# Moving pieces of a weight load and the bias loads to other places in the DMA queues of a fused attention and MLP kernel

## The chip, the cores and the metric

The kernel runs on one core of a Trainium2 chip. The metric is the device time of one execution in microseconds (us); the time of a kernel is the median of its runs. The core has five engines with queues of their own: TensorE (PE, with its weight loads shown as PEld), VectorE (DVE), ScalarE (ACT), GpSimd (POOL) and SyncE (SP). In this kernel SP issues nearly all DMAs; ScalarE issues a few.

## The reference

The kernel computes a gated mix of two branches over one sequence of S = 2048 rows with D = 512 columns, all in bfloat16. The first branch is linear attention with 32 heads of 16 columns; the second mixes tokens with a two-layer MLP of F = 1792 hidden units along the sequence.

```python
def _A_ref(x, wqkv, wo):                    # x [1, 2048, 512]
    q, k, v = ...                           # x @ wqkv, split in 32 heads of 16
    phi = lambda t: jnp.where(t > 0, t + 1, jnp.exp(t)) + 1e-6
    pq, pk = phi(q), phi(k)
    kv = jnp.einsum("bhsd,bhse->bhde", pk, v)
    z = jnp.einsum("bhsd->bhd", pk)
    num = jnp.einsum("bhqd,bhde->bhqe", pq, kv)
    den = jnp.einsum("bhqd,bhd->bhq", pq, z)[..., None] + 1e-6
    return merge_heads(num / den) @ wo

def _B_ref(x, w1, b1, w2, b2):              # w1 [2048, 1792], w2 [1792, 2048]
    h = _layernorm(x, axis=-1)
    u = _gelu(jnp.einsum("bsd,sf->bdf", h, w1) + b1)
    y = jnp.einsum("bdf,fs->bds", u, w2) + b2
    return y.transpose(0, 2, 1)

g = _sigmoid((x * gate_w).sum(-1, keepdims=True))
out = g * a + (1 - g) * b                   # a = _A_ref(A_x, ...), b = _B_ref(A_x, ...)
```

The input B_x is not used: both branches read A_x.

## The kernel before, in words

The sequence is cut into NT = 16 tiles of 128 rows, D into ND = 4 blocks of 128, and F into NF = 14 blocks of 128. All is kept in SBUF and nearly every instruction is put in program order by hand (`pin`), so the order in the source is the order in each engine's queue. The helper `load` (L122) issues every DMA, by default on SP's queue, so in the profile all DMA issues stand at line L123; all matmuls go through `mm` and stand at L74.

The stages follow one another on TensorE.

1. **Start.** VectorE fills `eps_t` (L113) and GpSimd fills `b_rows` (L114), a tile of 32 rows that will take the biases b1 (14 rows of 128) and b2 (16 rows). ScalarE's queue issues the load of the first 128 columns of w1's first tile, and then a dummy Sqrt (L134) that brings in its table. SP issues x tile by tile, alternating with the tiles of `w1A`, the first 8 blocks of w1's columns; the two bias loads come after w1's tile 4. TensorE runs 18 warm-up matmuls on constants.
2. **Layer norm and the first 8 blocks of the MLP.** For each x tile, VectorE takes the statistics, ScalarE the square root (`sd`), VectorE the reciprocal and the normalised tile `xh`. TensorE accumulates 8 PSUM banks `accA` over the 16 tiles, 8 matmuls for each tile and w1 tile. After tile 8, VectorE turns `b_rows` into columns and casts them into `b1_sb` and `b2_sb`.
3. **phi(k) and G = x^T phi(k)**, 16 tiles, with the sums z of phi(k).
4. **The other 6 blocks of the MLP** (`mlp1_block`, reading `w1B`) between the 16 tiles of q (`q_tile`), whose phi goes to `pq`. At its start SP issues the first half of w2 into the buffer of w1A. The gelu of each block gives `uT`.
5. **normalise(t)**: four VectorE instructions for each tile of phi(q), 12 of them in a row and the last four later; it divides by the denominator, weights with the gate's odds, and ends with a store of the tile to DRAM (`q_dram`). **turn(c)** loads four tiles (a group) back transposed, in four transposing DMAs, into `pqT`. Both issue on SP. The second half of w2, `load_w2(1, ...)`, goes into the buffer of w1B, so it can't start before TensorE has finished stage 4's last block. It is issued in four pieces right after the store of tile 0.
6. **Output**: for each tile t, 14 matmuls of `uT` with w2 (`y_mm`, tiles 0 to 7 from w2's first half, 8 to 15 from the second) and 4 matmuls of `pqT` with the folded output weights (`a_mm`) accumulate in one PSUM bank `yps`. The order on TensorE is y_mm of tiles 0 to 7, a_mm of 0 to 7; then y_mm and a_mm of 8 to 11; then of 12 to 14; and tile 15 last, in two parts. `finish` scales on ScalarE (tile 15 on VectorE) and stores.

The buffers tie the stages together: `w1A` and w2's first half share one tag, `w1B` and w2's second half the other. PSUM has 8 banks under one tag, `ot` (the output tile) has 6 buffers.

Of the kernel before, what the change touches and what calls it, by code (L numbers as in the profile page):

```python
# [15 lines left out]
def kernel(  # L16
# [13 lines left out]
    nc = tc.nc  # L30
# [10 lines left out]
    NT = S // P  # L41
    ND = D // P
    NF = F // P
# [12 lines left out]
    b1_view = B_b1.rearrange("(f p) -> f p", p=P)  # L56
    b2_view = B_b2.rearrange("(t p) -> t p", p=P)
# [8 lines left out]
    def ptile(shape, dt, name):  # L66
        return persist.tile(shape, dt, name=name, tag=name)
# [27 lines left out]
    b_rows = ptile([32, P], BF16, "b_rows")  # L95
# [14 lines left out]
    z_cols = ptile([P, ND], FP32, "z_cols")  # L110
    eps_t = ptile([P, 1], FP32, "eps_t")

    nc.vector.memset(eps_t[:], EPS)  # L113
    nc.gpsimd.memset(b_rows[:], 0.0)  # L114


    w1A = wpool.tile([P, NT, FA], BF16, name="w1A", tag="w1st")
# [4 lines left out]
    def load(o, i, eng=None, **kw):  # L122
        pin((eng or nc.sync).dma_start(out=o, in_=i, **kw))  # L123

    def load_x(t0, t1):
        load(xr[:, t0:t1, :], x_view[:, t0:t1, :])

    def load_w1a(t):
        load(w1A[:, t, :], w1_view[:, t, 0:FA])


    tbl = work.tile([P, 1], FP32, name="tbl", tag="tbl", bufs=2)
    load(w1A[:, 0, 0:P], w1_view[:, 0, 0:P], nc.scalar)
    pin(nc.scalar.activation(out=tbl[:], in_=eps_t[:], func=ACT.Sqrt))  # L134

    load_x(0, 1)
# [2 lines left out]
    for t in range(1, NT):  # L139
        if t + 1 < NT:  # L140
            load_x(t + 1, t + 2)
        load_w1a(t)
        if t == 4:
            load(b_rows[0:NF, :], b1_view)
            load(b_rows[NF : NF + NT, :], b2_view)
    load(gw_b[:], gw_row_view.to_broadcast([P, D]))
    load(wk_sb[:], wqkv_view[:, :, D : 2 * D])
    for c in range(NSC):
# [240 lines left out]
    def normalise(t):  # L389
        heads = by_head(pq[:, t, :])  # L390
        pin(
            nc.vector.tensor_tensor(  # L392
                out=prod[:, :, 0:HEAD], in0=heads, in1=by_head(zb[:]), op=ALU.mult,
            )
        )
        den = work.tile([P, NH], FP32, name="den", tag="den", bufs=2)
        pin(nc.vector.tensor_reduce(out=den[:], in_=prod[:], op=ALU.add, axis=AX.X))  # L397
        rd = work.tile([P, NH], FP32, name="rd", tag="rd", bufs=2)
        pin(nc.vector.reciprocal(out=rd[:], in_=den[:]))  # L399
        pin(  # L400
            nc.vector.scalar_tensor_tensor(  # L401
                out=heads, in0=heads, scalar=odds[:, t : t + 1],
                in1=rd[:].unsqueeze(2).to_broadcast([P, NH, HEAD]),
                op0=ALU.mult, op1=ALU.mult,
            )
        )
        load(q_dram[t * P : (t + 1) * P, :], pq[:, t, :])

    def turn(c):
        for j in range(ND):  # L410
            load(
                pqT[:, j, c * SC : (c + 1) * SC],
                q_dram[c * SC : (c + 1) * SC, j * P : (j + 1) * P],
                transpose=True,
            )
# [33 lines left out]
    def load_w2(h, f0, n=7):  # L449
        if f0 == 0:  # L450
            w2s.append(wpool.tile([P, NF, S // 2], BF16, name="w2h", tag=("w1st", "w2nd")[h]))
        load(
            w2s[h][:, f0 : f0 + n, :],
            w2_view[:, f0 : f0 + n, h * (S // 2) : (h + 1) * (S // 2)],
        )
# [41 lines left out]
    pin(nc.vector.tensor_tensor(out=c2[:], in0=c1[:], in1=b2_sb[:], op=ALU.mult))  # L497


    for t in range(12):  # L500
        normalise(t)
        if t == 0:
            for f0, f1 in ((0, 3), (3, 7), (7, 10), (10, NF)):
                load_w2(1, f0, f1 - f0)
        if t % 4 == 3:
            turn(t // 4)

# [41 lines left out]
    t = NT - 1  # L551
# [35 lines left out]
```

## Time and profile before

| | |
|---|---|
| median of 3 runs | 164.61 us (164.06 to 164.76) |
| the profiled execution's own time | 164.17 us |
| its span in the profile | 162.4 us |
| TensorE busy | 157.3 us (97%) |
| VectorE busy | 119.0 us (73%) |
| ScalarE busy | 53.1 us (33%) |
| GpSimd busy | 1.3 us (1%) |
| bytes moved by DMA | 28.33 MB, mean 174 GB/s |
| TensorE's granted clock | 1.0 of full speed |

The profiled execution's time holds the span and 1.8 us around it. In what follows, a line of a timeline gives the start in us from the span's start, the length, the engine, the source line, the operation, output and input and a count; SPq and ACTq are the queues that issue DMAs, and the length there is that of the issue, not of the transfer. A bracket at the end of a line gives the idle time of the engine before it and what ended that. A line of the chain of waits gives start, length and what was under way. A line of the table of DMA issues gives output and input, the queue, a count, the size of one, and the us from issue to landing.

### The profile page before, as it was taken

The page shows a single profiled execution, that of the slowest core. Times are in us where ns is not written, and L with a number is a line of the kernel's source. Part 1 is how long each engine was busy: PE and PEld are TensorE (multiplying, and loading weights), DVE is VectorE, ACT ScalarE, POOL GpSimd, SP SyncE. Part 2 cuts the span into 40 slices and gives each one's busy share as a digit, 9 for nine tenths or more (in the row PEclk, how much of TensorE's full clock was granted, in tenths as well). Part 3 has the DMA queues.
Part 4 walks back from the last instruction along what each step waited for, and adds up shares of the span by engine and source line. Part 5 has one row for each costly group of instructions (what it writes and reads, how often), then busy time and mean ns, then how long its engine had stood idle before and what let it go on. Part 6 is the DMA issues. An engine that isn't in the chain of part 4 may idle for free.

```text
span 162.4 us, 2272 instructions
## 1 busy us (share of the span) xinstructions
PE 157.3 (97%) x820; PEld 72.8 (45%) x820; DVE 119.0 (73%) x278; ACT 53.1 (33%) x89; POOL 1.3 (1%) x9
## 2 busy tenths in 40 slices
PE   7899999999999999999999999999997999999993
PEld 5344444444444444444444444444442444444452
DVE  2998998979999997989886999999999950000002
ACT  3222227794432420444425960000016303160050
POOL 3000000000000000000000000000000000000000
DMA  3999989544599940239942018975535358434021
GB/s 100 329 300 305 323 288 196 105 97 98 104 323 399 300 138 23 72 60 344 407 140 64 0 40 298 405 290 69 161 86 140 97 128 265 127 81 145 0 97 32
DMA packets 36838, 28.33 MB, mean 174 GB/s; under 512 B 20444, under 2 KB 31196, under 8 KB 36828
## 3 DMA queue, kind: packets, MB, share of 16 engines
q1 hardware_dynamic: 36412, 27.91, 57.7%
q10 hardware_dynamic: 416, 0.30, 0.6%
q8 instruction: 6, 0.10, 0.3%
q14 instruction: 4, 0.03, 0.1%
HBM read 19.28 MB, written 4.46 MB: 146 GB/s over the span
## 4 chain that ended last, share of the span: by engine, by line
PE 71%; DVE 19%; DMA 4%; SPq 2%; issue 1%; ACT 1%; DVEq 0%
PE yps L74 21%; PE accA L74 17%; PE Gps L74 9%; PE accB L74 9%; PE kacc L74 9%; PE qacc L74 7%; DVE den L397 4%; DVE pq L401 4%; DVE prod L392 4%; SPq L123 2%; DVE rd L399 2%; DVE pq L288 2%; DMA pqT<-q_dram 2%; DMA xr<-in_A_x_dram 1%; DMA q_dram<-pq 1%
## 5 line engine op out<-in xcount | busy, mean ns | idle before, releaser
L74 PE MATMUL yps<-uT,w2h 128*128 128x512 bf16 (+2 forms) x238 | 49.2, 367 | 0.0
L74 PEld LDWEIGHTS <-w2h 128*128 128x128 bf16 x238 | 22.7, 98 | 26.0
L74 PE MATMUL accA<-xh,w1A 128*128 128x512 bf16 x128 | 27.8, 379 | 0.4 <-DVE xh L205 0.4
L524 ACT ACTIVATE ot<-yps,c,c 128x512 bf16<-128x512 f32 x15 | 11.6, 777 | 48.1 <-PE yps L74 40.3
L74 PE MATMUL accB<-xh,w1B 128*128 128x512 bf16 x96 | 21.5, 379 | 0.0
L531 DVE TENSOR_SCALAR ot<-yps,c,c 128x384 bf16<-128x384 f32 (+1 forms) x2 | 1.1, 544 | 26.7 <-PE yps L74 26.7
L74 PEld LDWEIGHTS <-w1A 128*128 128x128 bf16 x128 | 12.5, 98 | 15.6 <-DMA w1A<-in_B_w_dram 0.9
L74 PEld LDWEIGHTS <-xT 128*128 128x128 bf16 x128 | 12.4, 98 | 14.9 <-issue 0.2
L74 PE MATMUL yps<-W2sb,pqT 128*128 128x512 bf16 (+2 forms) x68 | 14.8, 367 | 1.0 <-DMA pqT<-q_dram 1.0
L74 PE MATMUL kacc<-wk_sb,xT 128*128 128x512 bf16 x64 | 15.8, 379 | 0.0
L74 PE MATMUL Gps<-pk,xr 128*128 128x512 bf16 x64 | 15.8, 379 | 0.0
L74 PE MATMUL qacc<-wq_sb,xT 128*128 128x512 bf16 x64 | 14.5, 380 | 0.0
L74 PEld LDWEIGHTS <-w1B 128*128 128x128 bf16 x96 | 9.4, 98 | 11.3
L281 ACT ACTIVATE e<-qacc 128x512 bf16<-128x512 f32 x16 | 9.6, 597 | 12.2 <-DVE kvbdT L429 4.6
L281 ACT ACTIVATE e<-kacc 128x512 bf16<-128x512 f32 x16 | 9.2, 598 | 12.7 <-DVE pk L288 6.8
L192 DVE BATCH_NORM_STATS2 stats<-xr 128x6 f32<-128x512 bf16 (+1 forms) x19 | 11.2, 590 | 2.5 <-DMA xr<-in_A_x_dram 2.5
L401 DVE SCALAR_TENSOR_TENSOR pq<-pq,odds,rd 128x512 bf16<-128x512 bf16 x16 | 12.0, 752 | 0.6
L283 DVE TENSOR_SCALAR e<-e 128x512 bf16<-128x512 bf16 x32 | 9.2, 287 | 3.9 <-ACT e L281 3.5
L397 DVE TENSOR_REDUCE den<-prod 128x32 f32<-128x544 f32 x16 | 11.5, 720 | 0.6
L288 DVE SCALAR_TENSOR_TENSOR pk<-kacc,e 128x512 bf16<-128x512 f32 x16 | 11.1, 692 | 1.0
L240 DVE CUSTOM_DVE_ANT_0 junk<-xr,gw_b 128x512 bf16<-128x512 bf16 x16 | 11.0, 690 | 0.7 <-DMA gw_b<-in_gate_w_dram 0.3
L288 DVE SCALAR_TENSOR_TENSOR pq<-qacc,e 128x512 bf16<-128x512 f32 x16 | 11.1, 692 | 0.6
(52 smaller groups left out, 95.2 us busy)
## 6 DMA issues: line engine op xcount, KB each, us to landing
w1A<-in_B_w_dram SPq DMA_DIRECT2D x15, 256.0 KB, 4.9
w2h<-in_B_w_dram SPq DMA_DIRECT2D x2, 1792.0 KB, 9.4
w1B<-in_B_w_dram SPq DMA_DIRECT2D x4, 768.0 KB, 8.1
xr<-in_A_x_dram SPq DMA_DIRECT2D x16, 128.0 KB, 4.6
q_dram<-pq SPq DMA_DIRECT2D x16, 128.0 KB, 1.8
w2h<-in_B_w_dram SPq DMA_DIRECT2D x2, 1024.0 KB, 8.8
out_dram<-ot SPq DMA_DIRECT2D x15, 128.0 KB, 1.8
w2h<-in_B_w_dram SPq DMA_DIRECT2D x2, 768.0 KB, 8.5
```

The lines of the kernel that those rows point to most:

```text
L74: nc.tensor.matmul(o, lhsT=lhsT, rhs=rhs, start=start, stop=stop, **kw)
L123: pin((eng or nc.sync).dma_start(out=o, in_=i, **kw))
L192: pin(nc.vector.bn_stats(out=stats[t][:, h, :], in_=xr[:, t, d0:d1]))
L240: nc.vector.tensor_tensor_reduce(out=junk[:], in0=xr[:, t, :], in1=gw_b[:], scale=1.0, scalar=0.0, op0=ALU.mult, op1=ALU.add, accum_out=gp ...
L281: pin(nc.scalar.activation(out=e[:], in_=acc[:], func=ACT.Exp))
L283: nc.vector.tensor_scalar(out=e[:], in0=e[:], scalar1=1.0, scalar2=PHI_EPS, op0=ALU.min, op1=ALU.add)
L288: nc.vector.scalar_tensor_tensor(out=o, in0=acc[:], scalar=0.0, in1=e[:], op0=ALU.max, op1=ALU.add)
L392: nc.vector.tensor_tensor(out=prod[:, :, 0:HEAD], in0=heads, in1=by_head(zb[:]), op=ALU.mult,)
L397: pin(nc.vector.tensor_reduce(out=den[:], in_=prod[:], op=ALU.add, axis=AX.X))
L399: pin(nc.vector.reciprocal(out=rd[:], in_=den[:]))
L401: nc.vector.scalar_tensor_tensor(out=heads, in0=heads, scalar=odds[:, t : t + 1], in1=rd[:].unsqueeze(2).to_broadcast([P, NH, HEAD]), op0= ...
L524: nc.scalar.activation(out=ot[:, d0:d1], in_=yps[:, d0:d1], func=ACT.Identity, scale=c1[:, t : t + 1], bias=c2[:, t : t + 1],)
```

## The change

Two parts.

The load of w2's second half is still four pieces, but they are cut at other places (f blocks 0-4, 4-7, 7-11, 11-14; before 0-3, 3-7, 7-10, 10-14), and they are issued at other places of SP's queue: two after the store of tile 0, one after the store of tile 5, and one after the store of tile 7 and turn(1).

The two bias loads go from SP's queue, behind w1's tile 4, to ScalarE's queue: b1 ahead of w1's first columns and b2 behind them, both ahead of the dummy Sqrt. The fill of `b_rows` goes from GpSimd to VectorE, ahead of the fill of `eps_t`.

```diff
+    nc.vector.memset(b_rows[:], 0.0)
     nc.vector.memset(eps_t[:], EPS)
-    nc.gpsimd.memset(b_rows[:], 0.0)
...
     tbl = work.tile([P, 1], FP32, name="tbl", tag="tbl", bufs=2)
+    load(b_rows[0:NF, :], b1_view, nc.scalar)
     load(w1A[:, 0, 0:P], w1_view[:, 0, 0:P], nc.scalar)
+    load(b_rows[NF : NF + NT, :], b2_view, nc.scalar)
     pin(nc.scalar.activation(out=tbl[:], in_=eps_t[:], func=ACT.Sqrt))
...
         load_w1a(t)
-        if t == 4:
-            load(b_rows[0:NF, :], b1_view)
-            load(b_rows[NF : NF + NT, :], b2_view)
...
+    pieces = {0: ((0, 4), (4, 7)), 5: ((7, 11),), 7: ((11, NF),)}
     for t in range(12):
         normalise(t)
-        if t == 0:
-            for f0, f1 in ((0, 3), (3, 7), (7, 10), (10, NF)):
-                load_w2(1, f0, f1 - f0)
         if t % 4 == 3:
             turn(t // 4)
+        for f0, f1 in pieces.get(t, ()):
+            load_w2(1, f0, f1 - f0)
```

## The prediction

> **What bounds the kernel now.** I read the page first: TensorE is busy 97% of a span of 162.4 us, and its row by slices dips only in the first two slices, in one slice near 122 us, and at the end. So a transfer matters only where TensorE stands idle. Next I read TensorE's own timeline around that dip.
>
> ```profile
> 120.24 4.26 PE L74 MATMUL yps<-W2sb,pqT 128*128 128x512 bf16 x19
> 125.54 2.98 PE L74 MATMUL yps<-W2sb,pqT 128*128 128x512 bf16 x13 [1.03 <-DMA pqT<-q_dram]
> 128.35 12.25 PE L74 MATMUL yps<-uT,w2h 128*128 128x512 bf16 x56
> ```
>
> The second line ends an idle time of 1.03 us, and its releaser is a transposed load of phi(q) (pqT). The 112 matmuls before it start 24.18 us apart in all (96.06 to 120.24), 0.216 us each; the 32 a_mm matmuls take 8.11 us (120.24 to 128.35) where 32 x 0.216 = 6.91 would do. The stall is therefore worth 1.20 us, and that is all the change can win here. The chain of waits says what the stall hangs on:
>
> ```profile
> 116.84 1.83 DMA q_dram<-pq
> 118.66 0.02 SPq L123
> ...
> 122.55 2.94 DMA pqT<-q_dram
> 125.49 0.05 issue
> 125.54 34.12 PE yps L74 x175
> ```
>
> Store 7 of phi(q), issued at 116.84, lands at 118.66; then SP issues turn(1), four transposes, and the fourth lands at 125.49, when TensorE goes on. From there TensorE works without a break to the end (34.12 us). SP's timeline shows why store 7 is that late although VectorE had finished its tile at 112.07 (the last step of normalise(7) in VectorE's timeline: 111.32, 0.75 long):
>
> ```profile
> 94.39 0.33 SPq L123 DMA_DIRECT2D q_dram<-pq  x1
> 96.26 2.49 SPq L123 DMA_DIRECT2D w2h<-in_B_w_dram  x4
> 98.85 3.46 SPq L123 DMA_DIRECT2D q_dram<-pq  x3
> 109.49 5.71 SPq L123 DMA_TRANSPOSE pqT<-q_dram  x4
> 115.30 1.98 SPq L123 DMA_DIRECT2D q_dram<-pq  x4
> 118.78 5.03 SPq L123 DMA_TRANSPOSE pqT<-q_dram  x4
> 123.86 2.04 SPq L123 DMA_DIRECT2D q_dram<-pq  x4
> 127.40 5.03 SPq L123 DMA_TRANSPOSE pqT<-q_dram  x4
> ```
>
> SP issues in order. Store 3 goes out at 101.98, but turn(0) starts at 109.49: the table of DMA issues gives that store 7.4 us to its landing, where a store with nothing ahead takes 1.8:
>
> ```profile
> q_dram<-pq SPq DMA_DIRECT2D x1, 128.0 KB, 7.4
> ```
>
> It queued behind the 3.5 MB of w2's second half, issued from 96.26 to 98.74; windows of 0.25 us show 400 to 410 GB/s from 98.5 to 108.0 and the stores' bytes last, to 108.9. So the four pieces delay turn(0), turn(0)'s issue (to 115.20) delays stores 4 to 7, and these delay turn(1).
>
> **The change, w2's pieces.** Before: store 0, four pieces, stores 1 to 3, turn(0), stores 4 to 7, turn(1). After: store 0, pieces f 0-4 and 4-7 (1024 and 768 KB), stores 1 to 3, turn(0), stores 4 and 5, piece 7-11 (1024 KB), stores 6 and 7, turn(1), piece 11-14 (768 KB), stores 8 to 11, turn(2). The count of DMAs and bytes is the same. I follow the queue.
> - First two pieces: still issued at 96.26, when block 13's matmuls let go of w1B. They are 1.84 MB. Summing the windows, before had moved 1.83 MB by 103.0, so they end there. Stores 1 to 3 follow; before they took 1.4 us of data (about 107.5 to 108.9) and turn(0) came 0.6 after. So turn(0) starts at 103.0 + 1.4 + 0.6 = 105.0, 4.5 us sooner.
> - turn(0) issues for 5.03 us, as turn(1) and turn(2) do, or 5.71 as it did itself (its third transpose took 1.93 where the others take about 1.2). SP is free at 110.1 or 110.8. Stores 4 and 5 (tiles ready at 104.5 and 107.0) take 0.5 each, so piece 7-11 goes out at 111.1 or 111.8, stores 6 and 7 by 112.6 or 113.2.
> - The moved piece now lies ahead of stores 6 and 7. Its price: the pieces at 96.26 and wq (512 KB, issued 57.12) reached full rate 2.0 to 2.2 us after issue. So 111.1 + 2.1 = 113.2, 1.05 MB at 0.41 MB per us is 2.5, hence 115.7; two stores' data 0.95 at the rate of those at the end of the queue; landing and issue 0.5 (118.25 to 118.78 before): turn(1) at 117.1, or 117.8 with the long turn(0). Bounds from rows: with no hold at all store 7 lands 1.8 after issue, turn(1) at about 114.4; with the 7.1 us to landing that the second piece had at 96.70, which had 768 KB ahead, turn(1) starts at 119.1 to 119.8, later than 118.78. I take the middle, since a lone load is nearest: wq landed in 3.9 us.
> - turn(1)'s fourth transpose lands 6.7 after its start, so the delay in TensorE is 1.20 less what turn(1) comes earlier, not under zero: 118.78 - 117.8 = 1.0 gained, or the whole 1.20 from 117.58 on. I take 1.1.
> [...]
>
> **What is late next.** Tile 8's matmuls begin at 127.15 once the stall is gone. Piece 11-14 is first read at f = 11, 11 x 0.216 later, 129.5. It is issued after turn(1), 122.2 to 123.5; by the same price (2.1, then 0.79 MB at 0.41, then 0.6) it lands at 126.8 to 128.1: covered by 1.4 us or more. Piece 7-11 lands near 116.4, ten us early. turn(2) now waits behind that last piece and starts at 127.2 to 129.0 (127.40 before), landing by 135.7; tile 8's a_mm needs it at 127.15 + 56 x 0.216 = 139.2. turn(3) slides by as much, to at most 141.4, landing by 148.8; needed at 139.2 + 16 x 0.216 + 42 x 0.216 = 151.8. Output stores behind turn(2) hold ot buffers as before; PSUM banks of tiles 6 and 7 are wanted only after 142.
>
> **The change, the bias rows.** Removed: two DMA issues on SP (0.76 us at 6.06) and GpSimd's fill of b_rows (0.19; the mask behind it is first used at 64). Added: a fill on VectorE ahead of eps_t, no such row; between eps_t's 0.06 and GpSimd's 0.19, both over by 1.1, while VectorE next works at 3.12. On ScalarE's queue the first bias load waits for that fill, and behind it stand w1's first columns, the second bias load and the table load. At 0.40 to 0.45 each: bias at 1.05, w1 at 1.5 (0.80 before), second bias at 1.9, table load 2.3 to 3.6, dummy Sqrt to 3.8; the first real one starts at 4.06, so 0.26 is left.
>
> ```profile
> 4.36 0.10 PEld L74 LDWEIGHTS <-w1A 128*128 128x128 bf16 x1
> 5.31 0.98 PEld L74 LDWEIGHTS <-w1A 128*128 128x128 bf16 x6 [0.85 <-DMA w1A<-in_B_w_dram]
> ```
>
> w1's first columns took 2.5 us to land; they now land at 4.0, and at 5.5 with the 4.0 us that the bias rows took at 6.45. The first matmul, at 5.05, waits for xh anyway, and the second for w1's other columns (5.31, issued on SP at 1.72, not moved). So nothing at the near end, and 0.4 us lost at the far end; nothing is gained, as both these waits stay. One more wait: each DMA waits for the eighth before it (w1's tile 2, issued 3.62, landed 4.1 later; the eighth after it left at 7.75). Now x tiles 3 and 4 and w1's tile 2 wait for the three loads on ScalarE's queue: x tile 4 goes out at 4.4 to 5.9 (1.9 and a landing of 2.5 to 4.0) instead of 4.09. bn_stats of tile 4 starts at 8.67, and TensorE reaches tile 4 near 12.1 against xh at 11.05: a microsecond of cover. I take zero.
>
> **The sum.** 1.1 us off the profiled execution's 164.17 us (span 162.4 and 1.8 around it): 163.1. That execution lies 0.44 under the median of 164.61, so for the median I say 163.5.
>
> **Rivals.**
> - The moved piece holds store 7 after all: turn(1) starts at about 118.8 again and the stall only stays, 164.5. For it: stores 1 to 3 took 7.4 to 9.8 us behind w2's bytes. Against: 3.5 MB stood there, 1 MB here, and turn(0) is 4.5 us sooner. It needs 1 us more than I gave.
> - Slower: the last piece lands late. It has left the front of the queue for a place behind turn(1), and TensorE needs it at 129.5, in every tile from 8 on. If it took 8.5 us (the median of the 768 KB pieces) from 122.2 to 123.5, it would land at 130.7 to 132.0, a stall of 1.2 to 2.5: with the 1.1 won, the middle is 0.7 slower, 165.3. It decides from a landing after 129.5, and outweighs the gain from 130.6. For it: no row shows such a load right behind transposes. Against: the 8.5 us rows had 1.8 MB and more ahead or beside them, and wq alone took 3.9.
> - The first columns of w1 land at 5.5: 0.4 lost at the start, 0.7 won in all, 163.9. For it: x and w1 tiles crowd the queues from 2.2 us on. Against: the same columns took 2.5 us beside x's first tiles.
>
> **How the numbers follow.** Forecast 0.58, piece holding store 7 0.22, last piece late 0.12, first columns late 0.08. A measurement of this kernel tells about 0.5%, 0.8 us, from no change. The forecast's 1.0 to 1.2 lies above it: faster 0.58. The first and third rivals lie within: same 0.30. The second: slower 0.12. The forecast's own range is 163.1 to 163.9 (medians of the runs before spread over 0.7). For 8 in 10 it has to take in 164.5 and part of the second rival: 163.0 to 164.9.
>
> **What would show it.** In the new trace: turn(0) near 105.0 (wrong if after 107), store 7 landed and turn(1) begun at 117.1 to 117.8, no idle time of TensorE over 0.2 us ahead of the a_mm of tiles 4 to 7, no wait for w2h at tile 8, turn(2) between 127 and 129, first matmul of accA at 5.05. A wait on w2h near 129.5, a first matmul after 5.3, or turn(1) at 118.8 or later would each prove its step wrong.

## The result and the profile after

The changed kernel's median is 163.12 us (162.82 to 163.65) against 164.57 for the kernel before; the ratio is 0.992, with a 95% interval of 0.990 to 0.995. The profiled execution took 162.94 us (before 164.17), its span is 161.2 (before 162.4). In the two profiles the difference is 1.2 us. A median here is over all executions of a kernel, a ratio over those at full granted clock alone; only for the kernel with two pieces ahead of store 6 below does that make a difference, since three of its eleven executions took 167.6 to 168.9 us at a mean clock of 0.980 to 0.989.

TensorE's timeline, at the place where the stall was:

```profile
120.22 7.07 PE L74 MATMUL yps<-W2sb,pqT 128*128 128x512 bf16 x32
127.12 12.25 PE L74 MATMUL yps<-uT,w2h 128*128 128x512 bf16 x56
```

The 32 a_mm of tiles 0 to 7 are now one piece, and tile 8 begins 6.90 us after the first of them (8.11 before). The stall of 1.20 us is gone, and nothing took its place: the chain of waits ends with a single piece on TensorE from tile 0's first matmul to the last tile, where before VectorE, a store and turn(1) stood in it.

```profile
89.30 6.91 PE accB L74 x32
96.21 62.22 PE yps L74 x306
158.42 0.04 DVEq L532
158.46 0.05 issue
158.51 0.41 DVE ot L532
```

SP's timeline shows how (start, length of the issue, count at the end):

```profile
96.24 0.94 SPq L124 DMA_DIRECT2D w2h<-in_B_w_dram  x2
97.28 5.01 SPq L124 DMA_DIRECT2D q_dram<-pq  x3
104.75 5.06 SPq L124 DMA_TRANSPOSE pqT<-q_dram  x4
109.90 1.00 SPq L124 DMA_DIRECT2D q_dram<-pq  x2
110.94 0.46 SPq L124 DMA_DIRECT2D w2h<-in_B_w_dram  x1
111.45 2.05 SPq L124 DMA_DIRECT2D q_dram<-pq  x2
117.21 5.04 SPq L124 DMA_TRANSPOSE pqT<-q_dram  x4
122.29 0.58 SPq L124 DMA_DIRECT2D w2h<-in_B_w_dram  x1
122.97 1.97 SPq L124 DMA_DIRECT2D q_dram<-pq  x4
129.64 5.04 SPq L124 DMA_TRANSPOSE pqT<-q_dram  x4
```

turn(0) starts at 104.75 (109.49 before), turn(1) at 117.21 (118.78), turn(2) at 129.64 (127.40). Store 3 lands 2.8 us after its issue instead of 7.4. From the table of DMA issues, store 3 and then the last piece of w2:

```profile
q_dram<-pq SPq DMA_DIRECT2D x1, 128.0 KB, 2.8
...
w2h<-in_B_w_dram SPq DMA_DIRECT2D x1, 768.0 KB, 5.8
```

The last piece, issued at 122.29, is there at 128.1; TensorE first wants it at 127.12 + 11 x 0.216 = 129.5.

At the start, the list of TensorE's weight loads:

```profile
4.42 0.15 PEld L74 LDWEIGHTS <-w1A 128*128 128x128 bf16 x1
4.95 1.39 PEld L74 LDWEIGHTS <-w1A 128*128 128x128 bf16 x7 [0.38 <-DMA w1A<-in_B_w_dram]
6.80 2.27 PEld L74 LDWEIGHTS <-w1A 128*128 128x128 bf16 x12 [0.46 <-DMA w1A<-in_B_w_dram]
```

The first matmul starts at 4.95 (5.05 before). That is no work of the change: with the bias loads at their old place it was 4.97 in one of the kernels below (w2's part alone), and 5.10 in the changed kernel run again. And there is now a second wait for w1, at tile 1 (6.80). kacc, the next stage, starts at 32.71 against 32.73, so nothing is won at the start.

### The profile page after: what moved, and what is told of

Its sections match the earlier page's. It is cut to its first block, busy times and chain, and to the rows that moved or that the text cites. A ratio compares the mean times of both kernels' runs of the same rounds, so it can differ in the third digit from the quotient of the medians.

```text
span 161.2 us, 2275 instructions
## 1 busy us (share of the span) xinstructions
PE 157.5 (98%) x820; PEld 73.0 (45%) x820; DVE 118.8 (74%) x279; ACT 53.0 (33%) x89; POOL 1.2 (1%) x8
## 4 chain that ended last, share of the span: by engine, by line
PE 95%; DMA 1%; DVE 1%; ACT 0%; issue 0%; DVEq 0%
PE yps L74 39%; PE accA L74 17%; PE accB L74 13%; PE qacc L74 9%; PE Gps L74 9%; PE kacc L74 9%; DMA xr<-in_A_x_dram 1%; DVE stats L192 0%; PE kvps L74 0%; DVE xh L205 0%; DVE ot L532 0%; PE w2ps L74 0%; ACT tbl L137 0%; ACT sd L197 0%; DVE mv L195 0%
## 5 line engine op out<-in xcount | busy, mean ns | idle before, releaser
L74 PE MATMUL accB<-xh,w1B 128*128 128x512 bf16 x96 | 21.5, 379 | 0.0
L74 PEld LDWEIGHTS <-w1B 128*128 128x128 bf16 x96 | 9.4, 98 | 11.3
```

The source lines that it names most:

```text
L74: nc.tensor.matmul(o, lhsT=lhsT, rhs=rhs, start=start, stop=stop, **kw)
```

## The experiments

**The two parts alone.** The kernel before, with the new places of w2's pieces only:

```diff
+    pieces = {0: ((0, 4), (4, 7)), 5: ((7, 11),), 7: ((11, NF),)}
...
-            for f0, f1 in ((0, 3), (3, 7), (7, 10), (10, NF)):
...
+        for f0, f1 in pieces.get(t, ()):
...
```

> The kernel before with the new places of w2's pieces alone; the bias loads stay where they were. My theory (the gain comes from turn(1) starting earlier, the bias loads are hidden in both places): turn(0) near 104.8, turn(1) near 117.2, no stall of TensorE ahead of the a_mm of tiles 4 to 7, 1.2 us less than before, about 163.4. The rival (a part of the gain, 0.2 to 0.4 us, comes from the bias loads, since the measured gain of 1.45 is more than the 1.20 of the stall): 0.8 to 1.0 us less than before.

Measured: 163.06 us, ratio 0.992 (0.989 to 0.995), turn(0) at 104.74, turn(1) at 117.55, no stall. No run here tells the pieces' new sizes from their new places. And the bias part only (the fill of `b_rows` moves to VectorE with it):

```diff
...
+    load(b_rows[0:NF, :], b1_view, nc.scalar)
     load(w1A[:, 0, 0:P], w1_view[:, 0, 0:P], nc.scalar)
+    load(b_rows[NF : NF + NT, :], b2_view, nc.scalar)
...
```

> The kernel before with the moved bias loads and fill alone; w2's pieces stay where they were. My theory: no change within 0.2 us (164.4 to 164.8), the stall of 1.2 us near 124 is still there, first matmul of accA between 4.9 and 5.1. The rival that gives the bias loads a share: 0.2 to 0.4 us less than before, 164.2 to 164.4. The rival that they cost: first matmul at 5.3 or later and 0.3 us more.

Measured: 164.43 us, ratio 1.000 (0.998 to 1.002). The stall is still there, in TensorE's timeline:

```profile
120.26 4.52 PE L74 MATMUL yps<-W2sb,pqT 128*128 128x512 bf16 x19
125.61 2.98 PE L74 MATMUL yps<-W2sb,pqT 128*128 128x512 bf16 x13 [0.82 <-DMA pqT<-q_dram]
```

So the gain is that of w2's pieces; the bias part is worth nothing within 0.2%. The rival that gave it 0.2 to 0.4 us finds no support, though the interval leaves room for about 0.3 us either way. The rival that they cost falls: the first matmul starts at 4.95. That the medians differ by 1.45 and the profiles by 1.2 is put down to spread between executions: w2's part alone gave 1.33, and the changed kernel run again (below) 1.29, each against the kernel before on its own chip.

**Bytes ahead of the stores.** Three kernels move the pieces alone, to tell which store's wait counts. First, piece 11-14 also ahead of stores 6 and 7:

```diff
-    pieces = {0: ((0, 4), (4, 7)), 5: ((7, 11),), 7: ((11, NF),)}
+    pieces = {0: ((0, 4), (4, 7)), 5: ((7, 11), (11, NF))}
```

> The changed kernel with the last piece (768 KB) moved ahead of stores 6 and 7, behind piece 7-11, so that 1.84 MB lie ahead of store 7 and not 1.05. My theory: 0.79 MB more at about 0.38 MB per us put 2.1 us on turn(1), which starts at 119.3; that is 0.5 after the 118.78 of before, so the stall is 1.7 us and the time 0.5 over before, 165.1. The rival (an early turn(0) is what counts, the pieces between the stores do not): turn(1) near 117.2, as fast as the changed kernel, 163.1.

Measured: 165.80 us, ratio 1.007 (1.004 to 1.010), slower than before (165.1 expected). Counted from tile 0's start, turn(0) is as early as in the changed kernel, and yet turn(1) is late:

```profile
120.45 5.04 SPq L124 DMA_TRANSPOSE pqT<-q_dram  x4
```

```profile
120.79 4.05 PE L74 MATMUL yps<-W2sb,pqT 128*128 128x512 bf16 x18
125.52 0.39 PE L74 MATMUL yps<-W2sb,pqT 128*128 128x512 bf16 x1 [0.68 <-DMA pqT<-q_dram]
126.97 2.98 PE L74 MATMUL yps<-W2sb,pqT 128*128 128x512 bf16 x13 [1.07 <-DMA pqT<-q_dram]
129.79 12.25 PE L74 MATMUL yps<-uT,w2h 128*128 128x512 bf16 x56
```

The stall is 129.79 - 120.79 - 6.91 = 2.1 us (1.7 expected). Direction and mechanism are as expected, the size is 0.4 short: in the two half microseconds from 116.0 to 117.0 the DMA engines moved only 152 and 225 GB/s, about where the second piece began, and I had counted a steady rate.

Next, three pieces behind store 0 and none between stores 5 and 6:

```diff
+    pieces = {0: ((0, 4), (4, 7), (7, 11)), 7: ((11, NF),)}
```

> The changed kernel with piece 7-11 issued with the first two behind store 0, so that nothing of w2 stands between stores 5 and 6. My theory: turn(0) starts 2.6 us later (1.05 MB at 0.4), near 107.4, its issue ends at 112.5, stores 4 to 7 follow at 0.5 each, store 7 lands 1.8 after its issue, turn(1) at 115.9, no stall: as fast as the changed kernel, 163.1. The rival (what counts is how early turn(0) starts): half of the gain is lost, 163.8.

Measured: 163.19 us, ratio 0.993 (0.991 to 0.996), turn(0) at 107.87, turn(1) at 116.94 (115.9 expected), no stall. Half the advance of turn(0) is lost and none of the time. And two pieces behind turn(1):

```diff
+    pieces = {0: ((0, 4), (4, 7)), 7: ((7, 11), (11, NF))}
```

> The changed kernel with piece 7-11 behind turn(1), just ahead of the last piece, so that nothing of w2 stands ahead of store 7. My theory: turn(1) near 114.1, piece 7-11 issued at 119.1 and landed by 124.7, the last by 126.8; TensorE reads them from 128.6 and 129.5 on, so there is no stall: 163.1. The rival (late pieces come too late): a wait of TensorE for w2h near 128.6 to 130 and 0.5 us or more over the changed kernel.

Measured: 163.17 us, ratio 0.993 (0.991 to 0.996). turn(1) at 115.18, 1.1 later than expected: store 7 took 2.7 us to land and not the 1.8 I had used, and turn(0) itself was 0.3 later in this trace (105.03). The two pieces landed at 126.1 and 128.5, later than the 124.7 and 126.8 expected, but ahead of their first readings at 129.0 and 129.9: no stall, and no wait for w2h.

The kernels' starts of tile 0's matmuls differ by up to 0.6 us between these traces. In the latest of them, that of two ahead of store 6, the first three matmuls of accA take 1.44 us together (the first five 1.24 in the changed kernel); the mean granted clock of that execution is 0.999, and why is not shown. So turn(0) and turn(1) are counted from tile 0's start here (start on SP's timeline less the first yps matmul on TensorE's; the stall is the 32 a_mm's time less 6.91):

| kernel | turn(0) | turn(1) | stall, us | median, us |
|---|---|---|---|---|
| before | 13.4 | 22.7 | 1.2 | 164.57 |
| bias part only | 13.4 | 23.0 | 1.2 | 164.43 |
| two ahead of store 6 | 8.7 | 23.8 | 2.1 | 165.80 |
| w2 part only | 8.6 | 21.4 | 0 | 163.06 |
| changed kernel | 8.7 | 21.2 | 0 | 163.12 |
| three at store 0 | 11.3 | 20.4 | 0 | 163.19 |
| two behind turn(1) | 8.6 | 18.7 | 0 | 163.17 |

The time goes with turn(1), not with turn(0): up to 21.4 there is no stall, and at 22.7 to 23.8 it grows from 1.2 to 2.1. Earlier than that buys nothing. The edge, turn(1) less the stall, lies at 21.5 to 21.8 (22.7 less 1.2, 23.0 less 1.2, 23.8 less 2.1), so the changed kernel stands only some 0.3 to 0.6 us before it.

**The same bytes on another queue.** The kernel before, with the four pieces at their old place in the program but issued from ScalarE:

```diff
...
-                load_w2(1, f0, f1 - f0)
+                load_w2(1, f0, f1 - f0, nc.scalar)
```

> The kernel before with the four pieces of w2's second half, at the old place in the program, issued on ScalarE's queue and not on SP's. It tells the order within one queue from the sharing of the DMA engines. If the stores were late because they stood behind w2's bytes in the same queue (my theory), store 3 now lands 2 to 4 us after its issue at 102.0, turn(0) starts between 104 and 106, turn(1) before 117.5, the stall is gone: 163.4. If it is the bytes as such, whichever queue they are on (the rival), store 3 still lands near 109 as the bytes end, turn(0) stays at 109.5, and the time stays at 164.6.

Measured: 163.37 us, ratio 0.993 (0.990 to 0.996), turn(1) at 117.19 and no stall, but neither account of it holds: turn(0) starts at 107.75, between the two. Store 3, in a queue with stores alone, still took this long (table of DMA issues):

```profile
q_dram<-pq SPq DMA_DIRECT2D x1, 128.0 KB, 5.2
```

against 7.4 before and 1.8 with nothing about. It was issued at 102.55 and landed at 107.75; the third piece, issued at 97.94 and 9.6 us to landing, came in at 107.54. Store 2 (100.02, 5.5 us) landed at 105.5, the second piece (97.39, 8.2 us) at 105.6. So a store on its own queue came in with the piece of w2 then under way, and the order of one queue is only a part of what held it. An even share of the 400 GB/s for each queue would be, as an estimate, 0.7 us for a store's 0.13 MB over the 1.8, not 5.2 or 5.5 to the landing. The trace, read by queue, shows when the bytes moved: from 98 to 105 SP's queue moved 283 packets, 0.26 MB, and from 105.0 to 105.6 five more, 0.00 MB. That is what stores 1 and 2 hold, so nothing of store 3 moved in the 3.0 us from its issue to 105.6, while the DMA engines moved 362 to 408 GB/s (half microseconds from 102.5 to 105.5), most of it ScalarE's (1.98 of 2.25 MB from 98 to 105). Its bytes came late, behind those of store 2. Why the stores' bytes moved so slowly beside ScalarE's queue stays open. ScalarE's fourth piece went out only at 105.52, so 2.6 MB lay ahead of turn(0) and not 3.7, which may have helped too.

**The last piece too late.** The changed kernel with piece 11-14 behind turn(2):

```diff
+    pieces = {0: ((0, 4), (4, 7)), 5: ((7, 11),), 11: ((11, NF),)}
```

> The changed kernel with the last piece behind turn(2) in place of turn(1): the rival of the late last piece, made true. My theory: turn(2) starts near 126.1 and is issued by 131.2, the piece lands 5.8 later, at 137.0; TensorE wants it at 129.5, so it stalls for 7.5 us at tile 8 and the time is 170.6. The last piece's cover in the changed kernel is then 1.4 us, as the landing at 128.1 says. If TensorE does not stall there, the piece had far more cover than that and the time stays at 163.1.

Measured: 172.5 us in a single execution. The piece left SP at 131.16 and took 5.1 us; TensorE's timeline:

```profile
127.29 2.54 PE L74 MATMUL yps<-uT,w2h 128*128 128x512 bf16 x11
136.33 12.61 PE L74 MATMUL yps<-uT,w2h 128*128 128x512 bf16 x44 [6.51 <-DMA w2h<-in_B_w_dram]
```

After exactly 11 matmuls TensorE stops, as the f index says, and waits until 136.33, when the piece lands. The delay is 136.33 - 129.67 = 6.7 us (7.5 expected). The rest is the clock. In the table by stretches the row ends with TensorE's granted clock, the DMA share and GB/s:

```profile
127.00:129.60 2.60, 2.60 (x13) 1.08 (x11) 2.50 (x5) 0.00 (x0) 0.00 (x0) 1.00 0.45 101
129.60:136.30 6.70, 0.23 (x2) 0.00 (x0) 2.74 (x5) 0.00 (x0) 0.00 (x0) 0.91 0.76 191
136.30:138.00 1.70, 1.67 (x4) 0.57 (x5) 0.00 (x0) 1.23 (x2) 0.00 (x0) 0.50 1.09 380
140.00:142.00 2.00, 2.00 (x6) 0.70 (x5) 0.00 (x0) 0.00 (x0) 0.00 (x0) 0.53 0.08 20
142.00:144.00 2.00, 2.00 (x11) 0.88 (x9) 0.00 (x0) 0.00 (x0) 0.00 (x0) 1.00 0.51 113
```

The clock is 1.00 up to the stall, 0.50 after it and 1.00 again by 142. From the means of the second row and the fourth (0.91 over 6.7 us, 0.53 over 2), each taken as one step between 1.00 and 0.50, it fell by estimate about 1.2 us before the stall's end, near 135.1, and came back near 141.9. The last matmul starts at 167.59 against 158.02 in the changed kernel, 9.6 later: 0.2 from the start of tile 0, 6.7 from the wait, and so 2.7 from the half clock. So the clock fell some 5.4 us after the beginning of this stall of 6.5 us and came back some 5.5 us after its end; what sets these times is not shown. In the stretches around the stall of 1.2 us in the kernel before (120 to 128) and that of 2.1 us with two pieces ahead of store 6 (118 to 130) the clock reads 1.00.

**The start.** With the stall gone, what TensorE still waits for is w1 at tiles 0 and 1. To compare on one chip, the changed kernel again:

> The changed kernel once more, to be compared on one chip with the next kernel: 163.1, ratio to before 0.992. My theory of the start: TensorE begins at 4.95 and waits 0.4 to 1.3 us in all for w1's columns of tiles 0 and 1 (0.8 in the first profile).

Measured: 163.36 us, ratio 0.991 (0.989 to 0.994). In the trace TensorE begins at 5.10, and its weight loads wait 0.6 us in all for w1. And with two pairs of loads swapped:

```diff
     load_x(0, 1)
-    load_x(1, 2)
     load(w1A[:, 0, P:FA], w1_view[:, 0, P:FA])
-    for t in range(1, NT):
+    load_x(1, 2)
+    load_w1a(1)
+    load_x(2, 3)
+    for t in range(2, NT):
```

> The changed kernel with two pairs of loads swapped at the start of SP's queue: the rest of w1's tile 0 ahead of x tile 1, and w1's tile 1 ahead of x tile 2. With the stall near 124 gone, what TensorE still waits for is w1's columns at tiles 0 and 1. My theory: these land about 0.45 us (one issue) sooner, the waits of TensorE's weight loads for w1A go under 0.3 us, and the time is 0.2 to 0.4 us less than the changed kernel's, 162.8. The rival: x tiles 1 and 2 come later by as much, layer norm's chain becomes the bound, TensorE waits for xh, and the time is the same or 0.2 more.

Measured: 164.23 us, ratio to before 0.998 (0.996 to 1.001): 0.87 us over the changed kernel, most of the gain lost. My theory falls. The waits for w1A are gone, as I said, but TensorE begins at 5.49 (5.10 in the trace of the changed kernel on the same chip), and VectorE's timeline says why:

```profile
3.63 0.18 DVE L197 BATCH_NORM_AGGREGATE mv<-stats 128x2 f32<-128x6 f32 x1
4.50 0.43 DVE L194 BATCH_NORM_STATS2 stats<-xr 128x6 f32<-128x256 bf16 x1 [0.68 <-DMA xr<-in_A_x_dram]
4.84 0.14 DVE L205 RECIPROCAL rstd<-sd 128x1 f32<-128x1 f32 x1
5.02 0.41 DVE L207 TENSOR_SCALAR xh<-xr,mv,rstd 128x512 bf16<-128x512 bf16 x1
```

In VectorE's fixed order the statistics of the first half of x tile 1 stand ahead of tile 0's last steps. x tile 1 now lands 0.7 us after VectorE is ready for it, and tile 0's reciprocal and xh, whose own data were long there, wait behind it. That is the rival's mechanism, but its price was 0.2 us at most, and the traces don't show where 0.87 comes from. The execution traced is the fastest of twelve (163.59), and its kacc starts at 33.37, ahead of the 33.49 in the trace of the changed kernel (163.72); both are counted on from accA's rows at 0.216 us a matmul. So the cause of the longer median stays open. No version here is clearly faster than the changed kernel.

## Why the prediction was right, point by point

The forecast was 163.5 us, and 163.1 for the profiled execution; measured were 163.12 and 162.94. The median lies at the near end of the forecast's range (163.1 to 163.9): the stall accounts for 1.20 of the 1.45 us between the medians, and what the rest is was not shown. The path that the forecast followed is the one the traces have.

- **What bounds the kernel.** The stall of 1.20 us was all that could be won, and it was what went: 6.90 us for the 32 a_mm, and a chain that is TensorE alone from tile 0 on.
- **turn(0) at 105.0**: 104.75. The sum of the windows (1.83 MB by 103.0), the stores' 1.4 and the landing's 0.6 held. The rate was less even than said: the windows of before show 238 to 369 GB/s from 99.5 to 101.0, and the 1.83 MB include that.
- **turn(1) at 117.1 to 117.8**: 117.21, and 117.55 with w2's part alone. turn(0) took 5.06, the short case; the long third transpose of before (its issue 1.93) did not come back there (1.26). With 117.21 the stall goes whole, so the 1.1 I took was 1.20.
- **The moved piece**: by rows it was to land near 116.4, and it did (issued at 110.94, 5.5 us to landing).
- **The last piece at 126.8 to 128.1**: 128.1, at the far end of the span given for it, with 1.4 us of cover. That it lies inside is partly luck: the far end was worked out for an issue at 123.5, and it was issued at 122.29, the near end. It took 5.8 us and not the 4.6 reckoned (2.1, 1.9 and 0.6), most of that since full rate came 3.2 us after issue and not 2.1. The kernel with that piece behind turn(2) shows that the cover is real and what its loss costs.
- **turn(2) at 127.2 to 129.0**: 129.64. This step was too early, by 0.6, and turn(3) at 143.71 went past the 141.4 given as its latest. The price for the last piece was 1.2 us too low, and stores 8 to 11 landed behind it; output stores then spread out too. Both had cover: turn(2) landed by 136.3 (129.64 and 6.7) against 139.2, and turn(3) by about 150.4 against the 151.7 at which tile 12's a_mm begins. The margin at turn(3) is now 1.3 us, where 3 were reckoned.
- **The bias rows at zero**: 1.000 (0.998 to 1.002) alone. The first bias load's issue took 0.64 and not 0.40, so w1's first columns went at 1.69 and not 1.5; they landed after 2.7, at 4.4, still ahead of 4.95. The table load ended at 3.85 and the dummy Sqrt ran to 4.07, so that it now stands in the chain of waits ahead of the first real Sqrt: VectorE, free at 4.17, goes on with its result at 4.29 (4.35 and 4.39 before). My cover of 0.26 was used up, at some 0.1 us. The prediction did not have the new wait for w1 at tile 1 either (0.46 us; with the bias part alone the weight loads wait 1.1 us for w1, in two places). Neither lengthened the stage: kacc starts at 32.71 and 32.76, against 32.73 before. x tile 4 went out at 4.08 (4.09 before) and not at 4.4 to 5.9, so the wait for the eighth DMA before it cost nothing there. That wait itself shows in more rows of the trace of before: x tile 4 left at 4.09 and landed 4.6 later, and the eighth after it, x tile 7, left at 8.66; w1's tile 3 left at 4.57 and landed 4.7 later, and w1's tile 6 left at 9.28.
- **The rivals.** The piece holding store 7 did not come true in the changed kernel, but does with 0.79 MB more ahead of that store (165.80). The late last piece is 1.4 us away. The late first columns did not come.

## What to carry to other kernels

Find the transfer that the busy engine really waits for, and follow the queue it stands in backwards: here a store of 128 KB waited for megabytes that nobody needed for 30 us. Put a large load that is wanted late behind the small transfers that are wanted soon, in pieces, and reckon for each piece both ends: whom it holds up, and when it is itself first read. Once the stall is gone, more room buys nothing, and the next limit must be looked for elsewhere: here, moving loads at the start took away TensorE's wait for w1 (0.6 us) and brought one on VectorE (0.7 us).

## What the runs showed of the hardware

- In the changed kernel the first and third pieces of w2's second half, with nothing of their kind ahead, needed about 2 us from issue to full rate (96.24 to 98.3, 110.94 to 113.0), the last one 3.2. A slow patch came at its start: the windows from 123.5 to 125.5, after its issue at 122.29, show 12 to 66 GB/s while the DMA engines' share is 0.3 to 2.4, and then 389. A like patch, 152 and 225 GB/s from 116.0 to 117.0, stood about where the second piece began in the kernel with two ahead of store 6. Its cause was not tried.
- Stores on a queue of stores alone still took 5.2 and 5.5 us beside a stream of loads on another queue, and came in with the pieces under way there. In that kernel another queue shortened store 3's wait (5.2 us against 7.4) and did not do away with it (1.8 with nothing about).
- A stall of 6.5 us on TensorE cost 2.7 us more than its length, by a granted clock of 0.50 until about 141.9; stalls of 1.2 us (before and with the bias part alone) and 2.1 us (two pieces ahead of store 6) cost their length alone: from tile 8's first matmul to TensorE's last one 30.90 us pass in all three traces, as in the changed kernel.
